# Windowed attention into an expert layer on one core: visits of eight blocks, stretches of 512 tokens, three value banks, a ring for the bridge

## The chip, the core and the metric

The kernel runs on one core of one Trainium2 chip. A core has TensorE (matmuls, PE in the profile; its weight loads are PEld), VectorE (DVE), ScalarE (ACT), GpSimd (POOL) and SyncE (SP), each with its own instruction stream, and 16 DMA engines that move data between HBM and the on-chip memory SBUF. Matmuls write into PSUM: eight banks, each holding 512 fp32 values in each of 128 partitions. The metric is the time of one execution on the device in microseconds (us). The time before is the median of three runs, 296.31 us (295.82 to 296.36).

## The reference

Eight batches of eight heads, 576 positions, head size 64. Each position attends to itself and the 63 before it. The heads' outputs are put side by side (512 values a token, 4608 tokens) and go through two matrices with a SILU between them.

```python
scores = scale * np.matmul(q, k.transpose(0, 1, 3, 2))
rel = pos[:, None] - pos[None, :]
mask = (rel >= 0) & (rel < 64)
scores = np.where(mask, scores, -1000000000.0)
attn = np.exp(scores - np.max(scores, axis=-1, keepdims=True))
attn = attn / (np.sum(attn, axis=-1, keepdims=True) + 1e-09)
out = np.matmul(attn, v)                      # (8, 8, 576, 64)
x = out.transpose(0, 2, 1, 3).reshape(4608, 512)
h = x @ w_in                                  # (4608, 2048)
return (h * (1.0 / (1.0 + np.exp(-h)))) @ w_out
```

## The kernel before

**Attention.** Positions are cut into blocks of 64, nine a batch, 72 in all. The eight heads are two groups of four ("quads"). A *visit* takes one quad and some consecutive blocks. For each block TensorE makes the scores of 64 queries against 128 keys with eight small matmuls (line L261, one head to each quarter of the rows; four PSUM banks, the tile `at`). ScalarE takes the exponential in two halves of two heads each (L267, tile `e`), VectorE multiplies the mask in (L272), and TensorE multiplies with the values (L283): the values carry a column of ones, so that 65 columns come out, the last one the sum. The blocks come out in halves of 32 queries, so a visit of seven blocks fills 14 units of 65 columns; a bank holds seven of them. `norm` (L291 reciprocal, L292 multiply) divides, once for each bank, and `cross` (L295) transposes the visit's result into `bridge`, the input of the expert layer. In front of that, queries and keys are loaded by GpSimd's DMA queue (L219, four loads a batch), transposed by VectorE (`turn`, L237) into `qt` and `kt`, three batches deep; the values are loaded (L223, five loads a batch) and copied half a block up and down by VectorE (L244, L247). GpSimd issues its loads in order, so a load that waits holds up those behind it.

**Expert layers.** Tokens are worked in *stretches*. The first layer (L301) runs over 16 blocks of the hidden size and four parts of the 512 inputs, 64 matmuls a stretch, each as wide as the stretch; parts 0 and 1 come from quad 0, parts 2 and 3 from quad 1. ScalarE takes the SILU (L309) into `gate`, a ring of 1024 tokens; where a stretch goes over the ring's end, each SILU is two instructions. The second layer (L315) takes tiles of 128 tokens, 16 matmuls of 512 columns a tile, into one bank; the result is copied out (L319) and stored. The first 576 tokens (batch 0) are a piece of their own with small visits of three blocks; behind them come nine stretches of 448 tokens, one for each pair of visits of seven blocks (18 visits, numbered from 0). A stretch of 448 has three and four token tiles in turn.

**PSUM.** Four banks are `at`; the other four ("singles", tile `mp`) serve the expert layers one at a time (pool D) and the values two at a time (pools V and AV). The values of visits 0 and 1 go into `at` (`low`), since the second layer of batch 0 works on four token tiles at once.

**The order.** The class `Plan` writes out the whole program: a list of operations with an estimated duration, what each depends on, a rank, and queues by kind. It plays through time and gives each engine the operation of lowest rank that is ready; the order that comes out is the program, and the chip then waits only for the data. Expert matmuls (`moe`) have the highest rank number, so they fill what is left. Attention's matmuls come in *slots*: a slot holds the values of one visit and the scores of the next. Slots 0 and 1 are the scores of visits 0 and 1, slots 2 and 3 their values, slot 4 the scores of visit 2 alone, slot 5 values 2 and scores 3, slot 6 values 3 and scores 4, and so on; the last holds values alone. A slot also needs its PSUM banks free and, in the plan's count of words (instructions), room in TensorE's instruction buffer. `may_score` lets a slot in only while the second layer runs and more than eight of its matmuls are left, or when the next expert matmul isn't ready; `may_turn` lets the transposes of batch 4 and later run only beside the first layer. So in a steady stretch the order on TensorE is: first layer, slot, some 19 matmuls of the second layer, slot, the rest of the second layer. The two visits whose crosses come out of one stretch are the input of the next.

In the steady state slot 2k+3 holds values 2k and slot 2k+4 values 2k+1 (k from 1), and stretch k+1 begins with the first layer on them.

Of the kernel before, what the change touches and what calls it, by code (L numbers as in the profile page):

```python
# [14 lines left out]
class Plan:  # L15
# [13 lines left out]
    def add(self, cls, us, fn, deps=(), lat=0.08, gate=None, mb=None, pool=None, table=None, rank=None, words=2):  # L29
        op = dict(us=us, rank=self.rank[cls] if rank is None else rank, fn=fn, deps=[d for d in deps if d is not None],  # L30
                  lat=lat, gate=gate, mb=mb, pool=pool, table=table, seen=None, words=words, n=self.count, until=[], lower=[], bank=None, cls=cls)
        self.count += 1
        self.queues.setdefault(cls, []).append(op)
        return op
# [11 lines left out]
    def run(self, fillers=()):  # L46
# [9 lines left out]
        while left:  # L56
# [8 lines left out]
            while moved:  # L65
# [4 lines left out]
                for e in engines:  # L70
# [60 lines left out]
def kernel(ctx, tc, q, k, v, w_in, w_out, out):  # L131
# [12 lines left out]
    VB = 7  # L144
# [23 lines left out]
    bridge = keep.tile([128, NC, B * S], BF16, name="bridge")  # L168
# [5 lines left out]

    def bank(i):
        return at[:, i] if i < 4 else singles[i - 4]
# [3 lines left out]
         "V": [(i, j) for i in range(4, 8) for j in range(i + 1, 8)],  # L180
         "AV": [(0, 1, 2, 3, i, j) for i in range(4, 8) for j in range(i + 1, 8)]},
# [92 lines left out]
    def values(banks, n, quad, blocks):  # L274
        for s, g in enumerate(blocks):
            b, t = divmod(g, NB)
            vv = (vas if t % 2 else vbs)[b % NK][:, t // 2]
            for a in range(2):
                u = 2 * s + a
                c = u % VB * (D + 1)  # L280
                for j in range(4):
                    x = slice(32 * j, 32 * j + 32)
                    nc.tensor.matmul(  # L283
                        bank(banks[u // VB])[x, c:c + D + 1], lhsT=es[n % NE][:, j, 32 * u:32 * u + 32],
                        rhs=vv[:, 4 * quad + j, 0:D + 1], start=True, stop=True, tile_position=(0, 32 * j))

    def norm(banks, n, i, hi):
        lo = VB * i
        ps = bank(banks[i])[:, 0:(hi - lo) * (D + 1)].rearrange("q (u y) -> q u y", y=D + 1)
        rc = rcs[n % NO][:, lo:hi]  # L290
        nc.vector.reciprocal(out=rc, in_=ps[:, :, D])  # L291
        nc.vector.tensor_mul(obs[n % NO][:, lo:hi], ps[:, :, 0:D], rc.unsqueeze(2).to_broadcast([128, hi - lo, D]))  # L292

    def cross(n, quad, g0, nb):
        nc.vector.transpose(  # L295
            out=bridge[:, 2 * quad:2 * quad + 2, 64 * g0:64 * (g0 + nb)].rearrange("x c (u i) -> x c u i", i=32),
            in_=obs[n % NO][:, 0:2 * nb].rearrange("i u (x c) -> i c u x", c=2))


    def first_layer(bk, ft, c, lo, hi, at=0):  # L300
        nc.tensor.matmul(bank(bk["bank"][0])[:, at:at + hi - lo], lhsT=w_in_sb[:, c, ft * 128:(ft + 1) * 128],  # L301
                         rhs=bridge[:, c, lo:hi], start=(c == 0), stop=(c == NC - 1))
# [33 lines left out]
    def add_qk(b):  # L336
        for quad in range(2):
            for kk in (1, 0):
# [3 lines left out]
                               raw_free.get(w, []), MB * 4 * S * D, f"qk{b}.{quad}{kk}")]  # L342
# [47 lines left out]
    def add_slot(vals, scs, cls="slot", gate=None, low=False):  # L390
# [36 lines left out]
        for n in scs:  # L427
# [5 lines left out]
            for j0 in range(0, 4, split):  # L433
# [6 lines left out]
                exps.append(ex)  # L440
                op["lower"].append(ex)
            s0 += nb
        for k, n in enumerate(vals):
# [6 lines left out]
            for i in range(0, 2 * nv, VB):  # L450
                hi = min(2 * nv, i + VB)
                no.append(p.add("norm", {"DVE": 0.3 + 0.072 * (hi - i)},
                                lambda _, k=k, n=n, i=i, hi=hi: norm(banks(k), n, i // VB, hi),
                                [op] + o_free.get(n - NO, []), rank=None if t is None else RANK[(quad, t)]))
            op["lower" if low else "until"].extend(no)
# [6 lines left out]
    masked = {}  # L462
# [3 lines left out]
    def add_first(lo, hi, fts=range(NF), n=1, halves=False):  # L466
# [5 lines left out]
        for ft, c in order:  # L472
# [6 lines left out]
            moe.append((op, 1, 0, 0))  # L479
        for f0 in fts[::n]:  # L480
# [5 lines left out]
            for ft in range(f0, f0 + n):  # L486
                for g in range(lo // 64, hi // 64):
                    g_done[(g, ft)] = si

    g_done = {}  # L490

    def add_second(m0, m1):
# [7 lines left out]
        for i, (m, f, lo, hi) in enumerate(order):  # L500
# [5 lines left out]
            moe.append((op, 2, len(order) - i, 2 * m1 // VB - 1))  # L506
# [66 lines left out]
    seq = [new_visit(quad, list(range(NB + VB * i, NB + VB * i + VB)), 2) for i in range((B * NB - NB) // VB) for quad in range(2)]  # L573
# [48 lines left out]
```

## Time and profile before

| what | before |
|---|---|
| median of three runs | 296.31 us (295.82 to 296.36) |
| the profiled execution | 295.94 us, its span 294.2 us |
| TensorE busy | 281.7 us (96%), 3814 matmul records |
| VectorE, ScalarE, GpSimd busy | 128.2 us (44%), 173.7 us (59%), 64.4 us (22%) |
| first layer, 448 columns | 576 matmuls |
| exponential of 896, mask of 896 | 914 ns, 615 ns |
| SILU of 448, of 64 | 545 ns, 233 ns |
| granted TensorE clock | 1.00 |

A line of the profile's groups names the source line, the engine, the operation, what it writes and reads, its size and its count. The chain of waits is followed back from the last instruction: at each step to what released it. In its order of time each row is a start, a length and an engine with a line. In the timeline a bracket at the end of a row is idle time of the engine ahead of it and what ended it. Some matmul records are missing from the trace, so counts in it can be one or two short.

### The profile page before, as it was taken

Reading aid. Unit: us, or ns where it says so; the run is one execution under the profiler, and the core shown is the slowest. Engines: PE = TensorE matmul, PEld = TensorE weight load, DVE = VectorE, ACT = ScalarE, POOL = GpSimd, SP = SyncE. Lnnn points to the kernel's source line nnn. Section 1 sums busy time; section 2 is a strip of 40 time slices with the busy share of each in tenths; the row PEclk is TensorE's granted clock in tenths of the full one; section 3 lists DMA queues with packets and bytes.
Section 4 is the critical chain, followed back from the end, with each engine's and each line's share of the span. In section 5 each row is a group of like instructions: output and inputs, shape, how many; then the busy total and the mean of one; then the engine's idle time right before and its main releaser. Section 6 shows DMA issues by size and latency. Waiting matters only on the chain.

```text
span 294.2 us, 8531 instructions
## 1 busy us (share of the span) xinstructions
PE 281.7 (96%) x3814; PEld 150.0 (51%) x3838; DVE 128.2 (44%) x210; ACT 173.7 (59%) x320; POOL 64.4 (22%) x98
## 2 busy tenths in 40 slices
PE   7579999999999999999999999999999999999995
PEld 4347744555555545545554555455455545545444
DVE  4763567578763770791072059306304500530000
ACT  2566752875388467627864773686488338718512
POOL 6954566364330420250022000000000000000000
PEclk9999999999999999999999999999999999999999
DMA  6999999999993794197019001100100120010012
GB/s 114 151 192 206 205 183 198 252 188 212 134 220 28 80 181 71 38 149 185 0 44 148 2 3 74 71 0 30 48 36 2 57 87 4 2 74 36 0 74 72
DMA packets 51973, 28.34 MB, mean 96 GB/s; under 512 B 38880, under 2 KB 43360, under 8 KB 51936
## 3 DMA queue, kind: packets, MB, share of 16 engines
q0 software_dynamic: 46464, 18.36, 52.5%
q1 hardware_dynamic: 5472, 9.44, 8.7%
q8 instruction: 30, 0.49, 0.7%
q14 instruction: 7, 0.06, 0.1%
HBM read 36.70 MB, written 9.44 MB: 157 GB/s over the span
## 4 chain that ended last, share of the span: by engine, by line
PE 91%; DMA 5%; POOL 2%; issue 1%; ACT 0%; ACTq 0%; POOLq 0%
PE mp L315 42%; PE mp L301 41%; PE at L261 3%; PE mp L283 3%; DMA w_in_sb<-in_moe_w_in_dram 3%; DMA raw<-in_k_dram 2%; POOL va L223 1%; POOL w_in_sb L227 1%; PE at L283 0%; ACT ot L319 0%; POOL look L534 0%; ACTq L319 0%; POOLq L606 0%
## 5 line engine op out<-in xcount | busy, mean ns | idle before, releaser
L301 PE MATMUL mp<-bridge,w_in_sb 128*128 128x448 bf16 (+2 forms) x704 | 126.8, 340 | 1.8 <-DVE bridge L295 1.4
L315 PE MATMUL mp<-w_out_sb,gate 128*128 128x512 bf16 (+2 forms) x586 | 125.3, 368 | 2.3 <-issue 1.7
L309 ACT ACTIVATE gate<-mp 128x448 bf16<-128x448 f32 (+3 forms) x216 | 89.5, 460 | 23.6 <-PE mp L301 23.5
L301 PEld LDWEIGHTS <-w_in_sb 128*128 128x128 bf16 x704 | 67.8, 98 | 59.5 <-issue 1.5
L315 PEld LDWEIGHTS <-gate 128*128 128x128 bf16 x608 | 56.4, 98 | 62.2
L319 ACT COPY ot<-mp 128x512 f32<-128x512 f32 (+2 forms) x38 | 21.4, 564 | 69.5 <-PE mp L315 51.0
L291 DVE RECIPROCAL rc<-mp 128x7 f32<-128x7 f32 (+1 forms) x38 | 7.4, 194 | 105.6 <-PE mp L283 92.6
L223 POOL DMA_DIRECT2D va<-in_v_dram x40 | 34.0, 859 | 66.7 <-PE mp L283 58.0
L267 ACT ACTIVATE e<-at 128x896 bf16<-128x896 f32 (+1 forms) x42 | 35.6, 899 | 21.5 <-PE at L261 21.4
L272 DVE TENSOR_TENSOR e<-e,mask 128x896 bf16<-128x896 bf16 x36 | 21.7, 615 | 6.4 <-ACT e L267 5.7
L237 DVE STREAM_TRANSPOSE kt<-raw 128x576 f32<-128x576 f32 x16 | 19.8, 1237 | 9.7 <-DMA raw<-in_k_dram 9.6
L292 DVE TENSOR_TENSOR o<-mp,rc 128x448 bf16<-128x448 f32 (+1 forms) x38 | 23.3, 614 | 1.3
L295 DVE STREAM_TRANSPOSE bridge<-o 128x896 bf16<-128x896 bf16 (+1 forms) x24 | 23.4, 976 | 0.6
L237 DVE STREAM_TRANSPOSE qt<-raw 128x576 f32<-128x576 f32 x16 | 19.9, 1242 | 0.8 <-DMA raw<-in_q_dram 0.5
L283 PEld LDWEIGHTS <-e 128*32 128x32 bf16 x1152 | 10.8, 95 | 9.0 <-issue 7.6
L261 PE MATMUL at<-qt,kt 32*128 32x64 bf16 x1152 | 12.8, 189 | 1.0 <-DVE qt L237 1.0
L261 PEld LDWEIGHTS <-kt 32*128 32x128 bf16 x1152 | 10.7, 92 | 3.9 <-issue 3.2
L267 ACT ACT_TABLE_LOAD x9 | 11.5, 1283 | 0.8 <-PE at L261 0.6
L283 PE MATMUL mp<-vb,e 128*32 128x65 bf16 x576 | 10.9, 195 | 0.9 <-ACT e L267 0.6
L219 POOL DMA_DIRECT2D raw<-in_k_dram x16 | 9.0, 562 | 12.3 <-DVE kt L237 6.3
L309 ACT ACT_TABLE_LOAD x9 | 11.5, 1283 | 0.2
L283 PE MATMUL mp<-va,e 128*32 128x65 bf16 x464 | 10.3, 195 | 0.1
(41 smaller groups left out, 61.0 us busy)
## 6 DMA issues: line engine op xcount, KB each, us to landing
out_dram<-ot SPq DMA_DIRECT2D x35, 256.0 KB, 2.2
raw<-in_k_dram POOLq DMA_DIRECT2D x16, 288.0 KB, 7.8
raw<-in_q_dram POOLq DMA_DIRECT2D x16, 288.0 KB, 8.7
va<-in_v_dram POOLq DMA_DIRECT2D x32, 128.0 KB, 7.9
w_in_sb<-in_moe_w_in_dram POOLq DMA_DIRECT2D x8, 256.0 KB, 8.7
w_out_sb<-in_moe_w_out_dram POOLq DMA_DIRECT2D x8, 256.0 KB, 9.4
va<-in_v_dram POOLq DMA_DIRECT2D x8, 64.0 KB, 5.9
out_dram<-ot SPq DMA_DIRECT2D x1, 128.0 KB, 1.7
```

What stands on the lines that cost most here:

```text
L223: nc.gpsimd.dma_start(out=vas[b % NK][0:n, i, :, 0:D], in_=v[b, :, 128 * i:128 * i + n].rearrange("h p d -> p h d"))
L237: nc.vector.transpose(out=t.rearrange("x s c -> x (s c)").bitcast(FP32).rearrange("x (p y) -> x y p", p=32), in_=raws[w].bitcast(FP32).rea ...
L261: nc.tensor.matmul(at[:, j, 64 * s:64 * s + 64], lhsT=kts[b % NK][x, quad, 64 * t:64 * t + 128, r], rhs=qts[b % NK][x, quad, 64 * t:64 * t ...
L267: nc.scalar.activation(out=es[n % NE][:, j0:j1, 0:64 * nb], in_=at[:, j0:j1, 64 * s0:64 * (s0 + nb)], func=ACTF.Exp, scale=scale)
L272: (nc.gpsimd if e == "POOL" else nc.vector).tensor_mul(t, t, mask.unsqueeze(1).unsqueeze(1).to_broadcast([128, j1 - j0, nb, 64]))
L283: nc.tensor.matmul(bank(banks[u // VB])[x, c:c + D + 1], lhsT=es[n % NE][:, j, 32 * u:32 * u + 32], rhs=vv[:, 4 * quad + j, 0:D + 1], star ...
L292: nc.vector.tensor_mul(obs[n % NO][:, lo:hi], ps[:, :, 0:D], rc.unsqueeze(2).to_broadcast([128, hi - lo, D]))
L295: nc.vector.transpose(out=bridge[:, 2 * quad:2 * quad + 2, 64 * g0:64 * (g0 + nb)].rearrange("x c (u i) -> x c u i", i=32), in_=obs[n % NO ...
L301: nc.tensor.matmul(bank(bk["bank"][0])[:, at:at + hi - lo], lhsT=w_in_sb[:, c, ft * 128:(ft + 1) * 128], rhs=bridge[:, c, lo:hi], start=(c ...
L309: nc.scalar.activation(out=gate[:, ft:ft + n, x:x + m], in_=bank(bk["bank"][0]).rearrange("p (f x) -> p f x", f=n)[:, :, at:at + m], func= ...
L315: nc.tensor.matmul(bank(bk["bank"][0])[:, 0:hi - lo], lhsT=gate[:, f, x:x + 128], rhs=w_out_sb[:, f, lo:hi], start=(f == 0), stop=(f == NF ...
L319: copies[e](out=ots[ot][:, lo:hi], in_=bank(bk["bank"][0])[:, 0:hi - lo])
```

## The change

Visits take eight blocks (`VB = 8`): 63 blocks are seven visits of eight and one of seven for each quad, 16 visits in all. The stretches follow them: seven of 512 tokens and one of 448, each with four token tiles. A visit of eight blocks has 16 units; `parts` cuts them into banks of five, five and six (seven blocks: seven and seven). The pools V and AV now give out three of the four singles at a time, and each bank is given back by its own norm (`each`); before, both came back when both norms were done. The bridge is a ring: 576 columns for batch 0 and 2048 for the rest (`place`). `may_score` also lets the scores of visit 2 in during the last eight matmuls of the first layer of stretch 1, and their exponentials then wait for the last SILU of that stretch. The loads of queries and keys of batch 4 wait until slot 6 is done.

```diff
                     if op["pool"]:
                         op["bank"] = min((s for s in self.pools[op["pool"]] if self.free(s)), key=self.last)
+                        each = iter(op["each"])
                         for i in op["bank"]:
-                            self.banks[i] = (op["lower"] if i < 4 else op["until"]) or [op]
+                            self.banks[i] = (op["lower"] if i < 4 else next(each, op["until"])) or [op]
...
-    VB = 7
+    VB, UB, RB = 8, 7, 2048
...
-    bridge = keep.tile([128, NC, B * S], BF16, name="bridge")
+    bridge = keep.tile([128, NC, S + RB], BF16, name="bridge")
...
+    def place(x):
+        return x if x < S else S + (x - S) % RB
+
+    def parts(n):
+        k = -(-2 * n // UB)
+        return [2 * n * i // k for i in range(k + 1)]
...
-         "V": [(i, j) for i in range(4, 8) for j in range(i + 1, 8)],
-         "AV": [(0, 1, 2, 3, i, j) for i in range(4, 8) for j in range(i + 1, 8)]},
+         "V": [tuple(i for i in range(4, 8) if i != j) for j in range(4, 8)],
+         "AV": [(0, 1, 2, 3) + tuple(i for i in range(4, 8) if i != j) for j in range(4, 8)]},
...
     def values(banks, n, quad, blocks):
+        cut = parts(len(blocks))
...
-                c = u % VB * (D + 1)
+                at_bank = sum(u >= x for x in cut[1:])
+                c = (u - cut[at_bank]) * (D + 1)
...
-    def norm(banks, n, i, hi):
-        lo = VB * i
-        ps = bank(banks[i])[:, 0:(hi - lo) * (D + 1)].rearrange("q (u y) -> q u y", y=D + 1)
+    def norm(bk, n, lo, hi):
+        ps = bank(bk)[:, 0:(hi - lo) * (D + 1)].rearrange("q (u y) -> q u y", y=D + 1)
...
-            out=bridge[:, 2 * quad:2 * quad + 2, 64 * g0:64 * (g0 + nb)].rearrange("x c (u i) -> x c u i", i=32),
+            out=bridge[:, 2 * quad:2 * quad + 2, place(64 * g0):place(64 * g0) + 64 * nb].rearrange("x c (u i) -> x c u i", i=32),
...
-                         rhs=bridge[:, c, lo:hi], start=(c == 0), stop=(c == NC - 1))
+                         rhs=bridge[:, c, place(lo):place(lo) + hi - lo], start=(c == 0), stop=(c == NC - 1))
...
-    def add_qk(b):
+    def add_qk(b, held=[]):
...
-                               raw_free.get(w, []), MB * 4 * S * D, f"qk{b}.{quad}{kk}")]
+                               raw_free.get(w, []) + held, MB * 4 * S * D, f"qk{b}.{quad}{kk}")]
...
-        return (kind == 2 and rest > 8 and n <= 2 * unit + 2) or not p.done(op["deps"])
+        return (kind == 2 and rest > 8 and n <= 2 * unit + 2) or (unit == 1 and rest <= 8 and n == 2) or not p.done(op["deps"])
...
-            for i in range(0, 2 * nv, VB):
-                hi = min(2 * nv, i + VB)
-                no.append(p.add("norm", {"DVE": 0.3 + 0.072 * (hi - i)},
+            cut = parts(nv)
+            for i, (lo, hi) in enumerate(zip(cut, cut[1:])):
+                no.append(p.add("norm", {"DVE": 0.3 + 0.072 * (hi - lo)},
...
-            op["lower" if low else "until"].extend(no)
+            if low:
+                op["lower"].extend(no)
+            else:
+                op["each"].extend([x] for x in no)
...
-            moe.append((op, 1, 0, 0))
+            moe.append((op, 1, len(order) - i, unit))
...
-    seq = [new_visit(quad, list(range(NB + VB * i, NB + VB * i + VB)), 2) for i in range((B * NB - NB) // VB) for quad in range(2)]
+    stretch = [list(range(g, min(g + VB, B * NB))) for g in range(NB, B * NB, VB)]
+    seq = [new_visit(quad, gs, 2) for gs in stretch for quad in range(2)]
...
-                add_qk(loaded)
+                add_qk(loaded, p.queues["slot"][6:7] if loaded == 4 else [])
...
-    for hi in range(S, B * S + 1, 64 * VB):
-        if hi > S:
-            add_first(hi - 64 * VB, hi)
-        add_second((hi - 64 * VB) // 128 if hi > S else 0, hi // 128)
+    add_second(0, S // 128, 0)
+    for i, gs in enumerate(stretch):
+        lo, hi = 64 * gs[0], 64 * gs[-1] + 64
+        si = add_first(lo, hi, unit=i + 1)
+        if i == 0:
+            for ex in exps_of[seq[2]]:
+                ex["deps"].append(si)
+        add_second(lo // 128, hi // 128, i + 1)
```

More of the change, by code (lines that the diff above doesn't have):

```diff
@@ L30, in add @@
         op = dict(us=us, rank=self.rank[cls] if rank is None else rank, fn=fn, deps=[d for d in deps if d is not None],
-                  lat=lat, gate=gate, mb=mb, pool=pool, table=table, seen=None, words=words, n=self.count, until=[], lower=[], bank=None, cls=cls)
+                  lat=lat, gate=gate, mb=mb, pool=pool, table=table, seen=None, words=words, n=self.count, until=[], lower=[], each=[], bank=None, cls=cls)
         self.count += 1
@@ L283, in values @@
                     nc.tensor.matmul(
[L284 removed]
+                        bank(banks[at_bank])[x, c:c + D + 1], lhsT=es[n % NE][:, j, 32 * u:32 * u + 32],
                         rhs=vv[:, 4 * quad + j, 0:D + 1], start=True, stop=True, tile_position=(0, 32 * j))
[L287 to L289 removed]
+    def norm(bk, n, lo, hi):
+        ps = bank(bk)[:, 0:(hi - lo) * (D + 1)].rearrange("q (u y) -> q u y", y=D + 1)
         rc = rcs[n % NO][:, lo:hi]
@@ L440, in add_slot @@
                 exps.append(ex)
+                exps_of.setdefault(n, []).append(ex)
                 op["lower"].append(ex)
@@ L471, in add_first @@
             order.sort(key=lambda x: (x[0] - fts[0]) % n or x[1] // 2)
-        for ft, c in order:
+        for i, (ft, c) in enumerate(order):
             f0 = ft - (ft - fts[0]) % n
@@ L505, in add_second @@
             op["fn"] = lambda _, bk=bk, r0=r0, f=f, lo=lo, hi=hi: second_layer(bk, r0, f, lo, hi)
-            moe.append((op, 2, len(order) - i, 2 * m1 // VB - 1))
+            moe.append((op, 2, len(order) - i, unit))
             for g in range(2):
```

9 lines of the change are left out of this document (5 added, 4 removed).

## The prediction

> **What bounds the kernel now.** I read the page first, then TensorE's own waits, then the chain of waits in order of time, and last VectorE's timeline around the one hand-over where the chain could pass to another engine. The first lines of the page and the slices of its second part:
>
> ```profile
> span 294.2 us, 8531 instructions
> PE 281.7 (96%) x3814; PEld 150.0 (51%) x3838; DVE 128.2 (44%) x210; ACT 173.7 (59%) x320; POOL 64.4 (22%) x98
> ...
> PE   7579999999999999999999999999999999999995
> ```
>
> From the fourth slice (22 us) to the last but one TensorE is never under 90% busy; VectorE and ScalarE have half their time free. The waits of TensorE, longest first:
>
> ```profile
> PE mp L315 <- issue: 1.7, 11, 0.2
> PE mp L301 <- DVE bridge L295: 1.4, 1, 1.4
> ```
>
> The 1.4 us lies at 16.6 to 18.0 us, in a part that the change leaves alone. The eleven short ones stand where a matmul record is missing. So no wait is there to be removed; only TensorE's own work can shrink, or a new wait can come. The chain in order of time (start, us, what) shows a stretch, and the starts of those that follow:
>
> ```profile
> 80.61 12.11 PE mp L301 x64
> 92.72 0.56 PE mp L283 x43
> 93.27 0.55 PE at L261 x51
> 93.82 0.32 PE mp L315
> ...
> 105.54 12.11 PE mp L301 x64
> ...
> 133.92 12.11 PE mp L301 x64
> ...
> 158.85 12.11 PE mp L301 x64
> ```
>
> First layer 12.11 us; then values (L283) and scores (L261) of one visit each, about 0.55 us apiece; then the second layer. A stretch with four token tiles takes 133.92-105.54=28.38 us, one with three 158.85-133.92=24.93 us: 3.45 us for 16 matmuls of 512 columns, 215.6 ns each. The first layer's 448 columns take 12.11/64=189.2 ns. The last view is VectorE's timeline before the first layer of stretch 1 begins at 51.57:
>
> ```profile
> 43.46 0.82 DVE L244 COPY vb<-va 64x2560 bf16<-64x2560 bf16 x1
> 45.68 0.20 DVE L291 RECIPROCAL rc<-at 128x7 f32<-128x7 f32 x1 [1.39 <-PE at L283]
> 45.92 0.62 DVE L292 TENSOR_TENSOR o<-at,rc 128x448 bf16<-128x448 f32 x1
> 46.46 0.19 DVE L291 RECIPROCAL rc<-at 128x7 f32<-128x7 f32 x1
> 46.69 0.62 DVE L292 TENSOR_TENSOR o<-at,rc 128x448 bf16<-128x448 f32 x1
> 47.34 1.11 DVE L295 STREAM_TRANSPOSE bridge<-o 128x896 bf16<-128x896 bf16 x1
> 48.38 0.18 DVE L291 RECIPROCAL rc<-at 128x7 f32<-128x7 f32 x1
> ...
> 50.02 1.11 DVE L295 STREAM_TRANSPOSE bridge<-o 128x896 bf16<-128x896 bf16 x1
> ```
>
> From 45.68 to 51.13 VectorE runs without a gap: norm and cross of visit 0, then of visit 1. TensorE needs visit 1's cross for the third matmul of the new stretch, at 51.57+0.38=51.95. This hand-over has 0.6 us to spare; no other one I found has so little.
>
> **The change part by part.** *Fewer visits.* 18 become 16, the blocks stay 63 for each head group. What disappears is the fixed cost of two joint slots. Values of three blocks take 0.29 us in the chain (the pieces at 21.71 and 22.27), of seven 0.55: 0.065 a block and 0.095 fixed, the same for scores. The first matmul after a slot takes 0.32 instead of 0.216: 0.106 more. A joint slot thus has 0.095+0.095+0.106=0.30 of fixed cost. From the other side: a three-tile stretch without its matmuls, 24.93-12.11-48x0.2156, leaves 2.47 us for two slots, 1.235 each, less 14x0.065: 0.325. If the cost per block is the spacing inside a group, 0.060, the fixed part is 0.37. I take 0.325: two of them, **-0.65** (-0.60 to -0.74), all of it on TensorE and so on the path.
>
> *Stretches of 512.* Seven of 512 columns and one of 448 in place of nine of 448: 7x64x0.2156+12.11=108.70 against 108.99, with the 512 pitch of the second layer; with a pitch of 215.8, the spacing inside a token tile, 108.79; with 216.0 it would be 108.88. I take **-0.20** (-0.11 to -0.29). What each matmul costs beside its columns is the disputed size: the two pitches give (215.8-189.2)/64=0.42 ns a column and 3 ns at zero columns, 64 matmuls fewer of which are the 0.20. The Trainium skill, "TensorE: Matmul & The Clock Gate", section Back-to-back issue gap, gives for a sustained stream 81 ns at 128 columns and 131 ns at 512, which is some 64 ns at zero columns; by that, 64 matmuls fewer would be an estimated 4.1 us and the time 292. This trace doesn't agree: its 512 columns take 215.6 ns in a sustained stream, so that time gets no chance below.
>
> *The hand-over into stretch 1.* Visits 0 and 1 grow to eight blocks, and their chain is the tight one. Norms: a norm of seven takes 0.78 to the next norm and 0.88 to the cross, two of them 1.66. For six the early norms show 0.16 and 0.56 (reciprocal, multiply) against 0.20 and 0.62; carried on to five: 0.60, and 0.79 for the six ahead of the cross. 0.60+0.60+0.79=1.99, so +0.33 a visit. Cross: 1.11 at 896, 0.58 at 384, so +0.13 at 1024. Two visits: 2x0.46=+0.92; values of visit 0 +0.06. When they start: scores 0 and 1 are 0.06 longer each, and visit 0's two exponentials (0.914 at 896, 0.808 at 768: about 0.1 more each) put scores 1 one matmul later, 0.216. That is 0.34 (0.12 to 0.77: no matmul later, or three). Cross 1 then ends at 51.13+0.92+0.06+0.34=52.45. After the cross that ended the 1.4 us wait TensorE took 0.2 us to start: 52.65. TensorE gets there at 51.57+4x0.06+2x0.216=52.24. **+0.42** (0.1 to 0.9). Nothing else is ready then: queries and keys of batch 2 are turned from 51.06, after the last cross.
>
> *Three banks instead of two.* A slot now leaves one of the four single banks to the expert layers until the norms give banks back. TensorE's next need is at the end of the token tile in progress, up to 3.45 us away. The first bank is free after values 0.61, start 0.08, norm of five 0.63, hand-over 0.1 to 0.2: 1.4 to 1.5 us after the slot's start, and the slot itself takes 1.33. At worst 0.25 each, when one matmul is left; I take 0, cover: the tile in progress. At the end of a first layer the slot wants three free banks: SILU of the last but one block ends 0.86-0.1-0.60=0.16 us before. With SILU in two pieces (448+64, in four stretches) it costs 0.1 to 0.2 more: 0 to 0.1 each.
>
> *Costs nothing.* SILU: 0.545 and 0.233 (the split ones) are 0.78 against 0.86 us of matmuls. The exponentials of visit 2 wait for the last SILU; their table load already stands behind it (64.34 after 63.72+0.54). Scores of visit 2 inside the last eight first-layer matmuls: the same 0.66 at another place; behind them on TensorE only matmuls of the same stretch. Loads of batch 4, held until visit 3's values (about 79), are four q/k and behind them on POOL's queue five v and then batch 5. At 7.8 us to land and 1.4 apart they are there by 91, turned (4x1.06) by 96, wanted at about 102; v at 127. The ring: a cross overwrites columns that a first layer read over 70 us before, so the new wait is over when it is met.
>
> *Sum:* -0.65-0.20+0.42=-0.43 against the profiled execution's 295.94 (span 294.2 and 1.74 around): 295.5. That execution was 0.37 under the median 296.31, so on the median **295.9** (-0.15%).
>
> **The rivals.** *A: no wait at stretch 1.* If values 0 start without delay and the norms of five cost less than their line, cross 1 keeps its 0.6 us. For it: 0.42 is a small difference of long sums. Against: VectorE has no gap from 45.68. It gives 296.31-0.85=295.5.
>
> *B: slower, visit 3 too late for stretch 2.* Visit 3's values start 11.58 us after the first layer of stretch 1 ends (75.26-63.68) and its cross ends at 79.88, 0.7 us before the next first layer at 80.61. Slots are now 256 instructions of TensorE instead of 224, and TensorE's 7652 instructions come in 30 packets (the third part of the page, 0.49 MB), some 256 at a time, so the plan may hold the slot back. With two slots of 1.33 and 13.8 us of matmuls the stretch lasts 16.5 us; values 0.61, norms 2.0, cross 1.24 and 0.3 between are 4.1 us. From a start at 12.8 us on, each us late is a us of wait, up to 3.7 when the slot has to wait until all matmuls are gone. For it: the slack before. Against: scores of visit 2 now come earlier, and no wait for instructions stands on TensorE after 22 us. It gives up to 299.6; decided at 12.8.
>
> *C: banks.* With one single bank left, TensorE could wait for a norm behind every slot: at most 0.25 from the rows above at each of 13 joint slots, 3.3 us, which gives 299.2. Against: the trace of before, with two banks left, shows no such wait. The Trainium skill, "Perfetto Trace Analysis", Optimization Strategy, says that a gap that comes again and again on the engine that should be saturated can mean too little PSUM for the next tile; no run here shows it yet.
>
> *D: a longer wait at stretch 1.* A turn of 1.24 us slips in ahead of visit 1's norm, if the data of batch 2 land by then: +1.24, 297.1. Against: its first keys land at 48.7, when the cross before that norm has begun.
>
> **How the numbers follow.** A measurement of this kernel tells about 0.2% (0.6 us) from no change, so faster means under 295.7, slower over 296.9. My forecast with its own bounds (295.4 to 296.5) has 0.55: 0.17 of that is under the line, 0.38 within. A 0.23, faster. B 0.12, three quarters slower. C 0.05 slower, D 0.05, mostly slower. Faster 0.40, same 0.42, slower 0.18. The range 295.3 to 297.0 leaves out B's and C's upper ends and a little below A.
>
> **What would show it.** Two slots fewer: 16 groups of values after 35 us in place of 18, each joint slot about 1.33 us. First layer: 13.8 us, 64 times. The hand-over: TensorE's waits name the bridge's cross near 52 us, about 0.4 us, and VectorE has no gap before it. Wrong if that wait is missing (A), if it is above 1 us or returns near 83.5 us (B), or if short waits for the norms follow the slots (C).

## The result: 1.1% slower, and the profile after

| | before | after |
|---|---|---|
| median | 296.31 us (295.82 to 296.51) | 299.78 us (299.60 to 300.54) |
| ratio | | 1.0109, 95% interval 1.0072 to 1.0145 |
| profiled execution, its span | 295.94, 294.2 us | 299.6, 297.9 us |
| TensorE busy | 281.7 us | 283.0 us |

The prediction was 295.9 us, at most 297.0. The first lines of the page of the kernel after, and the slices of TensorE and of its granted clock:

```profile
span 297.9 us, 8416 instructions
PE 283.0 (95%) x3740; PEld 144.8 (49%) x3774; DVE 131.2 (44%) x225; ACT 168.9 (57%) x313; POOL 64.9 (22%) x98
...
PE   6599999999699999999999999999999999999995
...
PEclk9869999999999999999999999999999999999999
```

TensorE has fewer instructions and is still the engine that is always busy, but the eleventh slice (74.5 to 81.9 us) has fallen to 6. The clock row shows a second thing: between 13.30 and 20.12 us the clock was granted at half, which it was not in the profile of before. TensorE's waits give the cause of the eleventh slice; the columns are the total in us, how often, the longest:

```profile
PE mp L326 <- issue: 3.4, 11, 1.8
...
PE at L271 <- issue: 0.8, 1, 0.8
```

"issue" means that TensorE waited for nothing that the profile shows: no data, no bank, no semaphore. Before, the same eleven short ones came to 1.7 us with 0.2 as the longest; now there is one of 1.8 and a new one of 0.8 at the scores (L271). The chain of waits in order of time (start, us, what) shows where, in the second layer (L326) of stretch 1:

```profile
72.86 0.65 PE mp L295 x53
73.50 0.62 PE at L271 x62
74.12 0.16 issue
74.28 1.67 PE mp L326 x7
75.95 1.84 issue
77.80 2.54 PE mp L326 x11
80.33 0.67 PE mp L295 x55
81.00 0.52 PE at L271 x46
81.53 0.82 issue
82.35 0.27 PE at L271 x11
```

Slot 5 (values L295, scores L271) starts at 72.86. Eight matmuls behind it (one record is missing: 0.16+1.67 is 8x0.2159+0.106) TensorE stops for 1.84 us; in slot 6, in the middle of the scores, for 0.82 us. Scores read data that have long been there, and the stop lies between two matmuls of one group: this is not a wait for data.

The time by stages, from the ends of TensorE's matmuls in the two traces:

| stage | before | after | difference |
|---|---|---|---|
| start to the end of batch 0's first layer | 35.10 | 35.70 | +0.60 |
| on to the end of stretch 1's first layer | 28.58 | 31.77 | +3.19 |
| second layer of stretch 1 | 16.93 | 19.57 | +2.64 |
| the rest, to the last matmul | 210.13 | 207.36 | -2.77 |

The second and the last row are mostly work that changed places: stretch 1 is wider, so its first layer takes 13.81 instead of 12.11, the scores of visit 2 (0.72 with the slower matmul behind them) now lie inside it, four slots of eight blocks have 0.31 more; 3.19-1.71-0.72-0.31 leaves 0.45 of waiting. The third row should have shrunk: 64 matmuls of 215.9 ns and two joint slots of 1.367 (measured below) are 16.55 us, and it took 19.57. So 3.02 us are lost there, and that is the result: 1.84 and 0.82 in the two stops, and some 0.17 for each of them that the chain books on the matmuls behind (11 of them take 2.54 there instead of 2.37, the scores around the second 0.79 instead of 0.62). The matmuls behind a stop aren't slower: they start 0.216 us apart as always. But the first of them shows its whole length, 0.38 us, of which its predecessor hides a part in a running stream. Counted from start to start, the two stops are 2.00 and 1.00. Summed up: +0.10 from the change's own terms (below), +3.02, +0.60 at the start; 3.72, and the spans differ by 3.7.

Most of the 0.60 at the start isn't the change's: *real_hold* (below), which is the same kernel up to there, ends that stage at 35.30 in an execution with a clock of 1.00 throughout, and before too has executions with a mean clock of 0.988. The remaining 0.20 is no more than scatter: the traces of the kernels below, whose TensorE does the same up to there, end that stage between 34.85 (*f7_hold*) and 37.35 us (*no_hold*). Since each profile shows one execution, I compare below what lies between the end of batch 0's first layer and the last matmul ("the rest of the trace": 255.64 before, 258.70 after).

### The profile page after: what moved, and what is told of

Same layout as the page of the kernel before. It is cut to its first block, busy times and chain, and to the rows that moved or that the text cites. A ratio compares the mean times of both kernels' runs of the same rounds, so it can differ in the third digit from the quotient of the medians.

```text
span 297.9 us, 8416 instructions
## 1 busy us (share of the span) xinstructions
PE 283.0 (95%) x3740; PEld 144.8 (49%) x3774; DVE 131.2 (44%) x225; ACT 168.9 (57%) x313; POOL 64.9 (22%) x98
## 4 chain that ended last, share of the span: by engine, by line
PE 87%; DVE 4%; DMA 3%; issue 2%; ACT 1%; POOL 1%; DVEq 0%; ACTq 0%; POOLq 0%
PE mp L312 42%; PE mp L326 39%; PE at L271 3%; PE mp L295 3%; DMA va<-in_v_dram 2%; DVE o L303 2%; DMA raw<-in_k_dram 2%; DVE bridge L306 1%; ACT e L277 1%; POOL va L233 1%; DVE vb L254 1%; ACT gate L320 0%; DVE rc L302 0%; PE at L295 0%; DVE vb L257 0%
## 5 line engine op out<-in xcount | busy, mean ns | idle before, releaser
L326 PE MATMUL mp<-w_out_sb,gate 128*128 128x512 bf16 (+2 forms) x589 | 125.4, 368 | 3.9 <-issue 3.4
L312 PE MATMUL mp<-bridge,w_in_sb 128*128 128x512 bf16 (+3 forms) x627 | 127.0, 359 | 1.0 <-DVE bridge L306 0.2
L320 ACT ACTIVATE gate<-mp 128x448 bf16<-128x448 f32 (+2 forms) x216 | 88.6, 458 | 26.6 <-PE mp L312 26.3
L312 PEld LDWEIGHTS <-w_in_sb 128*128 128x128 bf16 x640 | 61.8, 98 | 64.3 <-issue 2.1
L326 PEld LDWEIGHTS <-gate 128*128 128x128 bf16 x608 | 56.7, 98 | 64.8 <-issue 2.1
L302 DVE RECIPROCAL rc<-mp 128x5 f32<-128x5 f32 (+2 forms) x46 | 8.6, 186 | 101.8 <-PE mp L295 101.8
L277 ACT ACTIVATE e<-at 128x1024 bf16<-128x1024 f32 (+2 forms) x38 | 35.1, 976 | 30.4 <-PE at L271 30.2
L233 POOL DMA_DIRECT2D va<-in_v_dram x40 | 34.8, 876 | 62.7 <-PE mp L295 55.2
L282 DVE TENSOR_TENSOR e<-e,mask 128x1024 bf16<-128x1024 bf16 (+1 forms) x32 | 21.1, 673 | 9.8 <-ACT e L277 9.5
L303 DVE TENSOR_TENSOR o<-mp,rc 128x320 bf16<-128x320 f32 (+2 forms) x46 | 24.3, 529 | 1.6
L306 DVE STREAM_TRANSPOSE bridge<-o 128x1024 bf16<-128x1024 bf16 (+2 forms) x22 | 23.1, 1049 | 0.5
L295 PEld LDWEIGHTS <-e 128*32 128x32 bf16 x1152 | 11.5, 97 | 8.5 <-issue 6.8
L271 PE MATMUL at<-qt,kt 32*128 32x64 bf16 x1152 | 12.9, 192 | 1.7 <-DVE qt L247 0.9
L271 PEld LDWEIGHTS <-kt 32*128 32x128 bf16 x1152 | 10.9, 93 | 4.9 <-issue 4.0
L295 PE MATMUL mp<-vb,e 128*32 128x65 bf16 x576 | 11.4, 198 | 0.9 <-ACT e L277 0.6
L295 PE MATMUL mp<-va,e 128*32 128x65 bf16 x448 | 10.5, 200 | 0.0
```

The source lines that it names most:

```text
L233: nc.gpsimd.dma_start(out=vas[b % NK][0:n, i, :, 0:D], in_=v[b, :, 128 * i:128 * i + n].rearrange("h p d -> p h d"))
L271: nc.tensor.matmul(at[:, j, 64 * s:64 * s + 64], lhsT=kts[b % NK][x, quad, 64 * t:64 * t + 128, r], rhs=qts[b % NK][x, quad, 64 * t:64 * t ...
L277: nc.scalar.activation(out=es[n % NE][:, j0:j1, 0:64 * nb], in_=at[:, j0:j1, 64 * s0:64 * (s0 + nb)], func=ACTF.Exp, scale=scale)
L282: (nc.gpsimd if e == "POOL" else nc.vector).tensor_mul(t, t, mask.unsqueeze(1).unsqueeze(1).to_broadcast([128, j1 - j0, nb, 64]))
L295: nc.tensor.matmul(bank(banks[at_bank])[x, c:c + D + 1], lhsT=es[n % NE][:, j, 32 * u:32 * u + 32], rhs=vv[:, 4 * quad + j, 0:D + 1], star ...
L306: nc.vector.transpose(out=bridge[:, 2 * quad:2 * quad + 2, place(64 * g0):place(64 * g0) + 64 * nb].rearrange("x c (u i) -> x c u i", i=32 ...
```

## What stops TensorE: the theories

**I, instructions.** The part of the page on DMA queues has a queue for instructions; the columns are packets, MB and share:

```profile
q8 instruction: 29, 0.48, 0.7%
```

Each packet is of 16,384 bytes. Counted in the trace, the second stop comes exactly 256 TensorE records behind the first (128 weight loads and their matmuls), and 29 packets for the program's some 7550 TensorE instructions are about 256 a packet. The kernels below stop on the same grid: their stops stand behind weight load 1248 (1247 in *seven* and *first7*), and where there are more, 128 and 512 loads further. So TensorE gets its program in blocks of 256, and it stopped at the ends of two of them. 256 records back from the first stop is the beginning of slot 5, at about 72.9. The DMA records show the packet that ends this stop starting at 75.54 and taking 0.88 us; TensorE went on at 77.80, 4.9 us after it had entered the block and 1.4 us after the packet's end. The next: entered at 77.80, packet at 79.97, on at 82.35, 4.55 us, again 1.4 us after the packet's end. All twelve such stops in the traces of this case, the short ones too, end 1.2 to 1.6 us after the end of a packet. A joint slot of eight blocks is 256 instructions and takes 1.37 us. It burns a block alone; behind it TensorE needs enough of the slow 512-column matmuls until the next block is there.

The Trainium skill, "Runtime: NRT & Kernel Launch", section Instruction fetch mechanics, says that instructions come in blocks of 16 KiB, 256 of them, over a DMA queue of the sequencer's own, and that the fetch is hidden by the pace of issue. The trace agrees on the block; that it is hidden is not so here, by 1.84 and 0.82 us.

What made the packets late? GpSimd's timeline of the kernel after (start, duration, what; in brackets the idle time ahead):

```profile
63.21 0.56 POOL L229 DMA_DIRECT2D raw<-in_k_dram  x1 [0.53 <-DVE kt L247]
...
72.72 0.56 POOL L229 DMA_DIRECT2D raw<-in_k_dram  x1 [0.42 <-DVE e L282]
```

The four queries and keys of batch 4 are issued at 63.21 to 66.92, then its values (67.79 to 72.3), then, at 72.72, batch 5: the DMA engines are full. But the change says that batch 4 waits for slot 6, and slot 6 began at 80.33. The edit puts the slot among the loads' dependencies in the *plan*. The loads and the slot share no data, so no semaphore comes out of it, and on the chip GpSimd just goes on. The plan, which delays a slot until it believes that TensorE has instructions enough, believed in a quiet DMA and put slot 6 only 19 matmuls behind slot 5; before, 26 matmuls lie between.

**The rivals**: H, that the loss is the hand-over into stretch 1 and what follows from it; C, the banks, as in the prediction; chance, that is the half clock of the profiled execution; and B in its own form, a slot held back and a cross that is late for stretch 2.

## Experiments

Ratios are against the kernel before in runs on the same chip.

**1. Make the hold real** (*real_hold*). GpSimd reads a result of visit 3's norms ahead of the loads, so that it waits on the chip too. The order of TensorE's instructions is the same as after.

```diff
+    def norm_3(b):
+        n = seq[3]
+        return [p.add("load", {"POOL": 0.2}, lambda _: nc.gpsimd.tensor_copy(out=look[0:1], in_=rcs[n % NO][0:1, 0:1]), norms_of[n])]
...
-                add_qk(loaded, p.queues["slot"][6:7] if loaded == 4 else [])
+                add_qk(loaded, norm_3(loaded) if loaded == 4 else [])
```

> The changed kernel, but the loads of batch 4 really wait: GpSimd first reads a reciprocal of visit 3. Theory I (late instructions): TensorE's stream comes in blocks of 256 instructions, a slot of eight blocks is one block, and the refill is late because the loads of batch 4 keep the DMA engines busy, although the plan holds them. With a quiet DMA the two waits of 1.84 and 0.82 us (at 76 and 81.5 us) fall to under 0.5 together: about 297.3 us. Theory C (banks): TensorE waits for the norms to give banks back; then nothing changes, 299.8.

Measured: 297.23 us, ratio 1.0023 [1.0003, 1.0043]. GpSimd's timeline and the chain of this kernel:

```profile
78.90 0.18 POOL L480 CAST look<-rc 1x1 bf16<-1x1 f32 x1 [17.37 <-DVE rc L302]
79.14 0.56 POOL L229 DMA_DIRECT2D raw<-in_k_dram  x1
```

```profile
73.82 1.67 PE mp L326 x7
75.50 0.21 issue
75.71 2.53 PE mp L326 x11
...
78.92 0.53 PE at L271 x48
79.44 0.27 issue
...
108.12 0.07 issue
```

The stops stand at the same instructions (behind eight matmuls, and inside the scores) and are 0.21 and 0.27 long. The packets start at 72.56 and 76.86, 0.2 and 1.1 us after their blocks were entered, where it was 2.7 and 2.2; they take 1.84 and 1.45 us. The table by windows of the two kernels shows what had changed around slot 5; the columns are the window and its length, then PE, PEld, DVE, ACT and POOL busy with counts, granted clock, DMA share (overlapping packets count twice, so it goes over 1) and GB/s. First after:

```profile
72.50:74.20 1.70, 1.62 (x130) 1.29 (x130) 1.64 (x3) 0.00 (x1) 0.67 (x2) 1.00 2.05 165
74.20:77.90 3.70, 1.78 (x8) 0.78 (x8) 3.60 (x9) 2.42 (x3) 0.44 (x1) 1.00 1.85 212
```

and with the hold made real:

```profile
72.50:74.20 1.70, 1.54 (x130) 1.32 (x120) 1.60 (x4) 0.46 (x1) 0.00 (x0) 1.00 0.29 94
74.20:77.90 3.70, 3.49 (x18) 1.46 (x15) 3.63 (x8) 1.96 (x3) 0.00 (x0) 1.00 0.21 75
```

The same 130 matmuls of slot 5, the same clock, the DMA share 0.29 instead of 2.05, and in the next 3.7 us TensorE does 18 matmuls instead of 8. That settles theory I: what stopped TensorE is the refill behind batch 4's and 5's loads. H falls too, since the hand-over into stretch 1 is the same in both traces (the third matmul starts 0.52 us behind the second). The rest of the trace takes 256.71, 1.99 less than after.

The kernel before, in the same windows, shows what the change took away:

```profile
72.50:74.20 1.70, 1.70 (x9) 0.78 (x8) 1.64 (x3) 0.59 (x1) 0.00 (x0) 1.00 1.67 209
74.20:77.90 3.70, 3.54 (x124) 2.10 (x124) 2.43 (x6) 1.42 (x2) 1.99 (x3) 1.00 1.25 144
```

Its loads of batch 4 go out at 63.03 to 66.73, the same time as after (batch 5 follows at 77.47, not 72.72), and its DMA engines are busy as well, with shares of 1.67 and 1.25. Its refill is late as well: counted on the same grid, the block in slot 5 is entered at 68.78, and the packet starts 3.6 us later. But the rest of the slot and 26 matmuls keep TensorE busy until 75.54, and only there does it need the next block. So the change didn't make the refill late; it took away the work that had covered it.

**2. No hold in the plan either** (*no_hold*). The plan now knows that the DMA is busy.

```diff
-                add_qk(loaded, p.queues["slot"][6:7] if loaded == 4 else [])
+                add_qk(loaded)
```

> The changed kernel without the hold of batch 4's loads in the plan. The plan then counts on a later refill and puts the slot of values 3 and scores 4 behind 39 matmuls of the second layer instead of 19, some two matmuls into the next first layer. Theory I: no wait for instructions at either slot, but a wait for visit 3's cross of 4.2-1.4=2.8 us near 85 us: 300.0 us. If the hold mattered through the DMA engines themselves: loads land as before, and the time falls with the waits to about 297.3.

Measured: 305.92 us, ratio 1.0316 [1.0255, 1.0376], far more than expected. TensorE's waits in this kernel, in the longest of its four executions (308.69 us), which is the one that was profiled:

```profile
PE mp L312 <- DVE bridge L306: 6.0, 3, 4.0
PE mp L326 <- issue: 3.9, 10, 2.5
```

The plan does hold slot 6 back: all 39 other second-layer matmuls and two of the next first layer come before it, and TensorE waits 4.0 us for the cross ahead of stretch 2 (1.9 of the 6.0 lie in batch 0). That is rival B, as the prediction described it. The first stop for instructions (2.5) was not avoided, since it lies behind slot 5. VectorE's timeline shows that the cross has one delay more:

```profile
89.87 0.20 DVE L302 RECIPROCAL rc<-mp 128x5 f32<-128x5 f32 x1 [7.17 <-PE mp L295]
...
92.81 0.69 DVE L282 TENSOR_TENSOR e<-e,mask 128x1024 bf16<-128x1024 bf16 x1 [0.22 <-ACT e L277]
93.42 1.24 DVE L306 STREAM_TRANSPOSE bridge<-o 128x1024 bf16<-128x1024 bf16 x1
```

The norms wait for the values until 89.87, and two masks of visit 4 (91.90 to 93.50) stand ahead of the cross. Two stretches of half clock (81.09 and 94.75, 3.41 us each) add some 1.7 us apiece to this execution, by estimate. So the hold in the plan alone saves 6 us as against none; made real, it saves 2.5 more.

**3. Visits of seven again, all else of the change kept** (*seven*), with three banks, the ring and the hold in the plan.

```diff
-    VB, UB, RB = 8, 7, 2048
+    VB, UB, RB = 7, 7, 2240
```

> The changed kernel with visits of seven blocks and stretches of 448 (two of the three banks used; ring of 2240): all of the change but its size. Theory I: slots of 224 instructions outlast the refill nearly, waits for instructions under 1 us; no wait at the hand-over into stretch 1: 296.3 to 297.5. Theory C: a slot still takes three banks, so the waits of 2.7 us stay: 299.

Measured: 297.47 us, ratio 1.0027 [1.0001, 1.0052]. The chain:

```profile
71.98 3.83 PE mp L326 x17
75.81 0.49 PE mp L295 x39
76.30 0.52 issue
```

No wait for a norm stands in this trace, nor in that of after, where the values fill all three banks. So rival C is refuted: three banks given back singly cost nothing that the traces show. Slot 6 stands here 18 matmuls behind slot 5 too, and here too TensorE runs out, for 0.52 us instead of 2.66. It is the plan's place for the slot, and not the eight blocks alone; but the size of the slots decides how much.

**4. The short stretch first** (*first7*): stretch 1 is the one of seven blocks, so that the tight hand-over is as before.

```diff
-    stretch = [list(range(g, min(g + VB, B * NB))) for g in range(NB, B * NB, VB)]
+    stretch = [list(range(NB, NB + 7))] + [list(range(g, g + VB)) for g in range(NB + 7, B * NB, VB)]
```

> The changed kernel with the short stretch of seven blocks first instead of last (ring behind 1024 columns). The hand-over into stretch 1 should lose its 0.45 us as in the kernel before; the waits for instructions stay, since slots and loads stay: 299.3 us. If the hand-over costs nothing, 299.8.

Measured: 297.0 us, ratio 1.0025 [1.0003, 1.0047]. Stretch 1's first layer starts 16.472 us after the end of batch 0's, before it was 16.471: the wait of the hand-over is gone. The time is 2.3 us under what I had expected, because the stop for instructions is smaller:

```profile
75.48 0.27 PE mp L296 x18
75.75 1.03 issue
```

(L296 are the values here.) With visits 0 and 1 of seven blocks the program up to slot 5 is 60 instructions shorter, and the ends of its blocks fall elsewhere against the slots: the stop falls 18 matmuls and 18 recorded values behind slot 5, not eight matmuls behind it.

**5. The changed kernel again** (*after2*), for the scatter.

> The changed kernel once more, beside the others and beside the kernel before on the same chip. TensorE's clock was granted at half for one or two windows of 3.4 us in the first 20 us in every run of it so far, which costs some 0.6 us; the runs of the last call, of the kernel before too, show that it comes and goes. If it is chance, the ratio to before falls from 1.011 to about 1.009 (3.0 us: 2.7 of waits for instructions, 0.45 hand-over, less 0.35 saved); if it belongs to the change, the ratio stays 1.011.

Measured: 300.23 us, ratio 1.0110 [1.0077, 1.0143], with a mean clock of 1.00 in two of the runs. The interval holds 1.009 too, so the ratio alone doesn't decide; but the two runs with the full clock took 299.71 and 300.29 us. The half clock at the start isn't the loss. This time the first stop was longer, and something came behind it; the chain, and the table by windows:

```profile
75.73 2.35 issue
78.08 4.13 PE mp L326 x11
```

```profile
78.10:82.10 4.00, 4.00 (x11) 1.28 (x10) 0.10 (x1) 0.00 (x0) 0.00 (x0) 0.59 0.54 134
```

Eleven matmuls took 4.13 us, at 215.9 ns they are 2.37: the clock granted in those 4 us was 0.59. It was half from 78.86 to 82.27, so the throttle closed 0.8 us after TensorE was back from 2.35 us without work. The second stop is missing: the slow matmuls bring TensorE to the end of the block at 83.25, and the next packet had ended at 81.18. So the same code loses 3.0 us in one execution and 4.1 in the other.

**6. Both repairs** (*f7_hold*): the edits of 1 and 4 together.

> Both mends together: the short stretch first, and the loads of batch 4 really wait for visit 3. Theory I: waits for instructions under 0.5 us, no wait at the hand-over, 0.35 us saved by fewer slots and matmuls: ratio 0.999 to 1.001. If the saving is the 0.85 us that the prediction counted: 0.998 or less. If another wait takes their place: above 1.002.

Measured: 296.68 us, ratio 0.9997 [0.9977, 1.0017]. The rest of the trace: 255.31, 0.33 less than before.

**7. Values and scores apart** (*split*): in stretch 1 each joint slot becomes two, the scores at least 2.5 us behind the values in the plan, so that no 256 instructions come at once. The values of visit 3, on which the plan's hold rests, are then slot 7.

```diff
-                add_qk(loaded, p.queues["slot"][6:7] if loaded == 4 else [])
+                add_qk(loaded, p.queues["slot"][7:8] if loaded == 4 else [])
...
+        if vs in ([2], [3]):
+            add_slot([seq[i] for i in vs], [], gate=lambda: may_score(0))
+            v_slot = p.queues["slot"][-1]
+            add_slot([], [seq[i] for i in ss], gate=lambda n=ss[0], v=v_slot: v["seen"] is not None and p.now > v["seen"] + 2.5 and may_score(n))
+            continue
```

> The changed kernel, loads as they are, but in stretch 1 each slot of values and scores is cut in two, with 12 or more matmuls of the second layer between: bursts of 128 instructions instead of 256. Theory I: a block of 256 instructions lasts some 4 us instead of 1.5 to 3, so the waits of 2.66 us fall under 1 us though the DMA engines are as busy as before: ratio 1.004 to 1.006. If only the DMA traffic counts: the waits stay near 2.6 us, 1.009 or more.

Measured: 299.37 us, ratio 1.0090 [1.0054, 1.0125]. In the chain:

```profile
75.74 0.58 PE at L271 x55
76.32 0.74 issue
...
87.07 1.28 ACT L320
```

With the DMA as full as after (shares 2.22 and 1.75 in the two windows), the stops fell from 2.66 to 0.74 us, as theory I says. But the time stayed where the rival had put it, for another reason: the scores of visit 4 now end where SILU is due, the exponentials come between two SILUs, and ScalarE loads its table once more (the 1.28 us at 87.07); TensorE waits 0.85 for that, until 89.01. The two slots more also have two slower first matmuls, 0.1 each. I had not counted these.

**8. Banks of seven, seven and two units** (*cut772*), where the change has five, five and six, to see whether the cut makes the values dearer (the first point of the next section).

```diff
-        return [2 * n * i // k for i in range(k + 1)]
+        return [min(UB * i, 2 * n) for i in range(k + 1)]
```

> The changed kernel with a visit's 16 units cut into banks of 7, 7 and 2 instead of 5, 5 and 6. Values of eight blocks took 0.645 us instead of the 0.61 counted. If TensorE's pace of issue makes it (some 8 ns a matmul behind the first 44), it stays 0.645; if the change of bank does, it moves.

Measured, in one execution: 300.28 us; values 0.647 us a visit against 0.645. The sum stays, but inside the values something moves: with the cut of 5, 5 and 6 the matmuls come in fours up to the 51st and then singly, with this cut up to the 59th. So the cut has a part in it, and this run doesn't exclude the banks; both cuts use three of them. Here too the first stop is 2.11 us and a half clock follows: 11 matmuls took 3.74.

**9. f7_hold again** (*f7_hold2*), beside *late6*.

> Short stretch first and a real wait of batch 4's loads, once more, for a tighter interval. In the trace the time from the end of batch 0's first layer (35 us) to the end was 255.31 us against 255.64 before. If the 0.33 us are real: ratio 0.998 to 1.000, and the same 255.3 in the trace; if they were chance, 255.6 or more.

Measured: 296.01 us, ratio 0.9983 [0.9957, 1.0010]; the rest of the trace 255.30. Its chain (L327 second layer, L296 values, L272 scores) has both slots and no stop:

```profile
70.23 0.65 PE mp L296 x57
70.88 0.62 PE at L272 x59
71.49 0.16 issue
71.65 3.83 PE mp L327 x17
75.48 0.69 PE mp L296 x59
```

The 0.16 is the first matmul after a slot, which is in every kernel. The packets start at 71.20 and 75.67, beside the slots, on a quiet DMA. The two traces agree that this kernel is 0.33 and 0.34 us shorter than before; the times can't tell it from before, and it beats the changed kernel by 1.1 to 1.3% (1.0109 against 0.9997 and 0.9983).

**10. Slot 6 later in the plan** (*late6*): at least 6 us behind slot 5, which gives 28 matmuls between, with the hold in the plan alone.

```diff
-        add_slot([seq[i] for i in vs], [seq[i] for i in ss], low=0 in vs or 1 in vs, gate=lambda n=max(ss + [0]): may_score(n))
+        add_slot([seq[i] for i in vs], [seq[i] for i in ss], low=0 in vs or 1 in vs, gate=lambda n=max(ss + [0]), five=p.queues["slot"][5] if vs == [3] else None: may_score(n) and (five is None or p.now > five["seen"] + 6.0))
```

> The changed kernel, loads as they are, but the slot of values 3 and scores 4 stands 28 matmuls behind the slot before it instead of 19 (26 before the change). Theory I: the first wait (1.8 to 2.4 us, the block that slot 5 uses up alone) stays, the second (0.82) goes, since the matmuls between give the refill 1.9 us more; visit 3's cross comes later and TensorE waits some 0.7 us for it: 299 to 300 us. If the slot's own size doesn't matter but only its distance, both waits go: 297.5.

Measured: 302.48 us (299.60 to 303.97), ratio 1.0206 [1.0163, 1.0249], above what I had expected. The chain of the execution of 299.6:

```profile
75.70 1.91 issue
...
86.03 1.25 DVE bridge L306
```

The first stop stayed, the second is gone, and TensorE's waits name 1.0 us for the cross ahead of stretch 2: in this execution the 0.82 us of the second stop are exchanged for 1.0 at the cross. Why the other executions took 301.6 to 304.0 stays open, since none of them was profiled.

## Why the prediction was wrong, point by point

**Fewer visits, -0.65: mis-sized, -0.19.** A joint slot of eight blocks takes 0.645 (values) + 0.616 (scores) + 0.106 = 1.367 us, of seven 0.553+0.549+0.106 = 1.208. 18x1.208 = 21.74; 14x1.367+2x1.208 = 21.55. The block from seven to eight costs 0.159, and I had carried 0.130 on from visits of three. Nearly all of the excess is in the values: they grow by 0.092, the scores by 0.067, and the prediction had 0.065 for each. In the trace the small matmuls start in fours some 30 ns apart. The 64 scores do so to the end, and so do the 56 values of seven blocks; the 64 values of eight blocks leave the fours at the 52nd and then come one by one some 8.8 ns apart. Fourteen visits of this spend the fixed cost of a slot, 0.325 in the prediction, again. What makes the values leave the fours stays open: values of eight blocks go into three banks, those of seven into two, and *cut772*, which moved the place, has three banks too.

**Stretches of 512, -0.20: right.** 7x13.813+12.107 = 108.80 against 9x12.107 = 108.96: -0.16. Together with the slots -0.35; *f7_hold*, which has nothing else, shows -0.33 and -0.34 in its two traces.

**The hand-over, +0.42: right.** VectorE's timeline after, ahead of stretch 1:

```profile
46.62 0.20 DVE L302 RECIPROCAL rc<-at 128x5 f32<-128x5 f32 x1 [0.86 <-PE at L295]
...
48.69 1.25 DVE L306 STREAM_TRANSPOSE bridge<-o 128x1024 bf16<-128x1024 bf16 x1
...
51.90 1.25 DVE L306 STREAM_TRANSPOSE bridge<-o 128x1024 bf16<-128x1024 bf16 x1
```

From 46.62 to 53.15 it has no gap. From the first norm to the first cross are 2.07 us (1.99 predicted), the crosses are 1.25 (1.24). TensorE's wait is 0.45, some 0.1 of it ahead of values 0, where a copy of values (L254) ends late. The list of waits doesn't name the rest, as the prediction had it; it shows between the second and the third matmul of the stretch, which start 0.52 us apart instead of 0.22. *first7* removes it.

**Three banks, 0: right** as far as waits go: no trace shows one for a norm. Whether the third bank is what makes the values dearer stays open, as said above. Rival C is out by the row of waits and by *seven*.

**Rival D** did not come: the transpose of batch 2 starts at 53.07, behind the cross.

**The step that failed is "Costs nothing", in its sentence "Loads of batch 4, held until visit 3's values (about 79)".** I took the hold from the diff for a wait on the chip, and I put nothing for what it does to TensorE. In the kernel's own way of ordering, a dependency without shared data is only the plan's belief. The loads went out at 63, not 79, as they had before the change. What the belief did change is the order: slot 6 came 19 matmuls behind slot 5 instead of 26, with 256 instructions in each slot instead of 224. The refill of TensorE's instructions, which starts 2 to 4 us late behind those loads before and after, was no longer covered: +3.02 us. In later stretches two slots of 256 stand only 22 to 24 matmuls apart, and on a less busy DMA no stop came.

The hold made true wouldn't have saved the forecast either, because its sum has no term for the refill at all. The terms above give -0.19-0.16+0.45 = +0.10; the rest of *real_hold* is 1.07 longer than before, so 0.97 belongs to instructions even then. From start to start its first two stops are 0.38 and 0.45; a third (108.12) costs 0.23 in stretch 2, where the loads of batch 5 now lie. That is 1.06, so the account closes to 0.1.

**Rival B** had the block of 256 and the slots of 256, and yet pointed the wrong way: it made the plan hold the slot back. That takes a plan that knows of the traffic (*no_hold*). With a plan that doesn't, the slot came in time and the stream ran dry. The argument against it, "no wait for instructions stands on TensorE after 22 us", was true of before, and was no evidence for an order of instructions that ends its blocks elsewhere: before, slot 5's refill started at 72.38 and slot 6's at 76.48, with 26 matmuls between the slots to cover them. A refill 3.6 us late that is covered leaves no wait in the list.

## What to carry to other kernels

In a program as long as this one the instructions are a transfer as well (29 packets here): mark where in the stream each block of 256 ends, and give every burst of short instructions enough long ones behind it for a refill on a loaded DMA, here about 5 us. A dependency written into an order planner holds nothing back on the chip unless it ends in a wait there; read in the diff which engine waits, on which data. And a saving of 0.1% may rest on shifting such blocks, so an edit that only changes the count of instructions can cost ten times what it saves.

## What the runs showed of the hardware

- While GpSimd's loads filled the DMA engines (share 2.05 and 1.85 in the first), TensorE went on 4.9 and 4.55 us after it had entered the block before: the packet starts 2.7 and 2.2 us after that, takes 0.9, and TensorE goes on 1.4 us after its end. With the hold made real it went on after 3.3 and 4.0 us: the packet starts after 0.2 and 1.1 and takes 1.84 and 1.45, and again 1.3 and 1.4 us follow.
- The stops of 2.35 us (after2), 2.11 (cut772) and 2.5 (no_hold) were each followed, 0.6 to 1.2 us after their end, by 3.41 us of half clock; those of 1.84 and 1.91 were not. The half-clock stretches of the traces, but for the last at their ends, are 3.41 us long or twice that. The Trainium skill, "TensorE: Matmul & The Clock Gate", section What's actually happening, speaks of a free-running window of some 3.4 us for the throttle; the traces agree with that length. So a stop near 2 us can cost 1.4 (cut772) to 1.8 us (after2) more. That its place in the window decides is my reading; no run here varies it.
- 512 columns take 215.9 ns a matmul, 448 take 189.2, in streams of 64. The straight line through the two leaves 2 to 3 ns at zero columns, an estimate.
